# Copying x from the attention tile into the gated layer's ring instead of reading it back from DRAM

## The chip, the cores and the metric

One core of one Trainium2 chip runs the whole kernel. The metric is the device time of one execution in microseconds. TensorE (PE) multiplies matrices, VectorE (DVE), ScalarE (ACT) and GpSimd (POOL) work element by element, SyncE (SP) issues nearly all DMAs. A profile of one execution goes with the times; its line numbers (L508) are those of the kernel file.

## What is computed

```python
# q, k, v: 4 batches x 8 heads x 576 x 64, f: 4 x 8 x 576
cum = np.cumsum(np.log(np.clip(f, 1e-4, 1.0)), axis=-1)
scores = q @ k.T / 8 + cum[:, None] - cum[None, :]       # per head, causal mask
attn = softmax(scores) @ v
x = attn.transpose(0, 2, 1, 3).reshape(2304, 512)
h = (sigmoid(x @ w_gate) * (x @ w_val)) @ w_out           # 512 -> 1536 -> 512
h2 = h @ w_in2                                            # 512 -> 2048
out = (h2 * clip(h2 + 3, 0, 6) / 6) @ w_out2              # 2048 -> 512
```

## The kernel before

**Attention** goes over 16 pairs of heads: 4 batches of 4 pairs. A pair has four units (blocks of query rows), run in the order 1 to 4 in the first seven pairs and 4 to 1 in the later ones. For each unit the main loop issues `scores` (TensorE, L371 and L385), `expo` (VectorE and ScalarE, L392 and L400), one step later `norm` (GpSimd, L437), two steps later `flip` (transposes on TensorE, copies to `etA`, `etB` on ScalarE, L474) and three steps later `values` (TensorE, L494). `values` leaves the pair's x, transposed, 128 rows (two heads) by 576 tokens of one batch, in two SBUF tiles: `x0` the rounded high part (ScalarE, L498), `x1` the low part (VectorE, L499). Each of the two tags has two buffers. `store` then writes both to the DRAM tensors `x_d` (L503).

**The gated layer** works on chunks of 512 tokens (the last has 256). It takes x as four blocks of 128 rows, `xk[kc]` with `kc` 0 to 3. A block is just the x of one pair of heads: pair `hp` of a batch is block `kc = hp`. Every product is made of three matmuls, high x high (L508), high weight x low x (L509), low weight x high x (L510). `load_x` (L206) brings one block of one chunk, high and low part, from `x_d` into the next of six slots of `xr`, a ring in the tile `big`.

While attention runs, `Filler` interleaves part of the gated layer for chunks 0, 1 and 2 (`NCA = 3`): two of the six groups of 256 features (`NGA = 2`). Chunk c lies in batches c-1 and c: its tokens 512c to 512c + 512 begin 64c tokens before batch c does. The main loop calls `fill.load(p.b, p.hp + 1)` two steps after the pair's store, and `Filler.run` starts a chunk when its batch is done:

```python
        if t >= 5:
            p, s = units[t - 5]
            if s == p.order[-1] and t < len(units) + 3:
                fill.load(p.b, p.hp + 1)
```

`Filler.load` holds blocks back where an earlier chunk still needs the ring. After attention the other feature groups follow for all chunks (the second pass, which loads chunks 0 to 2 again from `x_d`), and then the last layer.

**Order.** The loops write the program; the tile framework finds the dependences between accesses of tiles and DRAM tensors, and chooses at build time the order on each engine and queue from a planned timeline (`schedule_with_timeline_sim=True`). On the chip each engine and SP take their instructions in that fixed order. SP issues loads of q, k, v (L264, L268), of the decay (L302), of raw weights (L101), the x stores (L503), the x loads (L206) and the partial sums' stores (L594), and stands still where one has to wait.

Of the kernel before, what the change touches and what calls it, by code (L numbers as in the profile page):

```python
# [7 lines left out]
F32 = mybir.dt.float32  # L8
# [12 lines left out]
def attn_moe_kernel(  # L21
# [13 lines left out]
    nc = tc.nc  # L35
    B, H, S, D = q.shape
# [3 lines left out]
    P = 128  # L40
# [157 lines left out]
    xr = [big[:, 2 * T1 * i : 2 * T1 * i + 2 * T1].rearrange("p (a b) -> p a b", a=2) for i in range(6)]  # L198
    ring = {"x": 0, "g": 0, "s": 0}

    def load_x(src, c, kc):
        t0, T = chunks[c]
        x = xr[ring["x"] % len(xr)][:, :, :T]
        ring["x"] += 1
        for a in range(2):
            nc.sync.dma_start(x[:, a].bitcast(F32), src[a][kc * P : (kc + 1) * P, t0 : t0 + T])  # L206
        return x


# [26 lines left out]
    def row(mm, first):  # L236

        if not first:
            tc.keep_in_program_order(mm)
# [34 lines left out]
    class Pair:  # L274
# [202 lines left out]
        def values(self, part):  # L477


            if self.x is None:  # L480
                self.x = [ax.tile([P, S], F32R, tag=f"x{a}", name="x") for a in range(2)]
            c0, n, nk = (0, 256, 2) if part == 0 else (256, 320, NKT)
            pool, tag = (psF, "F") if FV(self) else (psB, "B")
            o = pool.tile([P, 512], F32, tag=tag, name="pv")[:, :n]
            for kt in range(nk):
                q0 = max(0, kt * P - c0)
                for j in range(2):
                    if part == 0:
                        e = self.etA[:, j, kt * 256 : 256 + kt * P]
                    elif kt < NQ:  # L490
                        e = self.etB[:, j, kt, q0:]
                    else:
                        e = self.etB[:, j, NQ - 1, 0:TAIL]
                    row(nc.tensor.matmul(  # L494
                        o[64 * j : 64 * j + 64, q0:], self.vn[:, kt, j], e, start=(kt == 0), stop=(kt == nk - 1)
                    ), kt == 0 and j == 0)
            xh, xl = (x[:, c0 : c0 + n] for x in self.x)
            nc.scalar.copy(xh, o)  # L498
            nc.vector.tensor_tensor(xl, o, xh.bitcast(F32), ALU.subtract)  # L499

        def store(self):
            for t, d in zip(self.x, x_d):
                nc.sync.dma_start(  # L503
                    d[self.hp * P : (self.hp + 1) * P, self.b * S : (self.b + 1) * S], t.bitcast(F32)
                )
# [38 lines left out]
    class Gated:  # L544
# [6 lines left out]
        def load(self, n):  # L551

            while len(self.xk) < n:
                self.xk.append(load_x(x_d, self.c, len(self.xk)))
# [94 lines left out]
    def layer(src, order, feats, ups, downs, finish, rate, first, more=None):  # L649
# [3 lines left out]
        def load(c, n):  # L653
            while len(loaded[c]) < n:
                loaded[c].append(load_x(src, c, len(loaded[c])))
# [383 lines left out]
    NGA, NCA, GA = 2, 3, 1  # L1039
# [27 lines left out]
    for t in range(len(units) + 3):  # L1067
        if 2 <= t < len(units) + 2:
            p, s = units[t - 2]
            p.flip(s)  # L1070
        if t < len(units):
            p, s = units[t]
            i = p.order.index(s)
            nxt = pairs[p.i + 1] if p.i + 1 < len(pairs) else None
            if i == 0 and nxt:
                nxt.load()
                nxt.load_decay()
                nxt.load_v()
            p.scores(s)
            p.expo(s)  # L1080
            if s > 1:
                p.hide(s - 1)
            if s == 2:
                p.hide(0)
            if nxt and i == (len(p.order) - 1 if p.up else 2):
                nxt.tail_decay()
        if 1 <= t <= len(units):
            p, s = units[t - 1]
            p.norm(s)
        if t < len(units) + 2:  # L1090

            fill.step(16 * (done + 1) + 3 - t + (TL if done == NCA else 0))
        if t >= 3:
            p, s = units[t - 3]
            if s in p.parts:
                p.values(p.parts[s])
            if s == p.order[-1]:
                p.store()
                if p.hp == NP - 1 and p.b < NCA:
                    done = p.b + 1  # L1100
# [5 lines that stand above are left out]
        if t < len(units):  # L1106
            p, s = units[t]
            if p.order.index(s) == max(0, len(p.order) - 3):
                if nxt:
                    nxt.prep()  # L1110
        if t >= C0:
            conv.run(CS if len(conv.jobs) <= 2 * NSA - 6 * NGA else CE if t < 16 else CA, EA)
        fill.n = done
    att.close()
    pace["dve"] = None
    psU = fu.enter_context(tc.tile_pool(name="psU", bufs=4, space=PSUM, reuse_waits="tile"))
# [60 lines left out]
```

## Time and profile before

| | us |
|---|---|
| median of 3 runs | 1041.06 (1040.39 to 1042.2) |
| profiled execution | 1043.08 |
| its span | 1041.0 |
| TensorE busy in it | 1021.1 |
| DVE, ACT, POOL busy | 571.4, 457.0, 307.6 |

The span is the profiled stretch from the first to the last instruction; the time of the execution holds some 2 us around it. Attention takes the first 314 us of it. Busy time of TensorE counts a matmul from its start to its modelled end, and neighbours overlap. A row "A <- B" in a list of waits says that A stood still until B was done.

### The profile page before, as it was taken

What the parts mean: (1) busy time and instruction counts of PE and PEld (TensorE: products, weight loads), DVE (VectorE), ACT (ScalarE), POOL (GpSimd) and SP (SyncE); (2) the same over time, 40 slices, a digit from 0 to 9 for tenths busy, and PEclk for the clock granted to TensorE, in tenths of its full rate; (3) what the DMA queues carried; (4) which work ended last, traced back from release to release, by engine and by line L of the source; (5) the groups of instructions that cost most, each with busy time, mean ns of one, the idle gap of its engine ahead of it and who ended that gap; (6) DMA issues with size and microseconds to landing.
All of it is one profiled execution on the core that took longest, in us unless ns stands there. A gap on an engine that the chain in (4) does not pass through costs nothing.

```text
span 1041.0 us, 15648 instructions
## 1 busy us (share of the span) xinstructions
PE 1021.1 (98%) x5410; PEld 837.0 (80%) x5410; DVE 571.4 (55%) x1282; ACT 457.0 (44%) x1004; POOL 307.6 (30%) x385
## 2 busy tenths in 40 slices
PE   7999999998999999999999999999999999999998
PEld 4656766765768888998888888888998998999997
DVE  5686655445434654456667267665655644443442
ACT  5786466456453443223334134353444432342333
POOL 4577555445432322030234123231111111111110
PEclk9999999999999999999999999999999999999999
DMA  7986666364334435184697458955589632952311
GB/s 184 269 246 196 178 182 180 108 173 116 100 121 139 128 123 158 57 276 176 260 344 244 150 183 293 353 196 211 224 311 338 255 146 79 341 206 81 142 71 61
DMA packets 118319, 197.79 MB, mean 190 GB/s; under 512 B 63648, under 2 KB 68256, under 8 KB 114144
## 3 DMA queue, kind: packets, MB, share of 16 engines
q1 hardware_dynamic: 118144, 196.64, 56.5%
q8 instruction: 43, 0.70, 0.3%
q14 instruction: 36, 0.29, 0.1%
q10 hardware_dynamic: 96, 0.15, 0.0%
HBM read 143.47 MB, written 53.29 MB: 189 GB/s over the span
## 4 chain that ended last, share of the span: by engine, by line
PE 90%; DMA 5%; DVE 2%; issue 1%; POOL 1%; ACT 1%; SPq 0%; POOLq 0%; DVEq 0%; ACTq 0%
PE po L510 11%; PE po L509 11%; PE po L508 11%; PE u L508 5%; PE u L509 5%; PE u L510 5%; PE pg L508 5%; PE pg L509 5%; PE pg L510 5%; PE pv L508 5%; PE pv L509 5%; PE pv L510 5%; PE pv L494 4%; PE st L371 3%; PE tt L461 2%; PE st L385 1%
## 5 line engine op out<-in xcount | busy, mean ns | idle before, releaser
L65 POOL TENSOR_TENSOR big<-tail,big 128x384 fp32r<-128x384 f32 x48 | 49.9, 1039 | 312.8 <-ACT big L62 299.4
L940 ACT ACTIVATE tail<-h,three 128x384 f32<-128x384 f32 x96 | 59.2, 616 | 157.9 <-DVE h L1000 157.0
L510 PE MATMUL po<-w,big 128*128 128x512 f32 x288 | 113.8, 395 | 0.0
L509 PE MATMUL po<-w,big 128*128 128x512 f32 x288 | 113.5, 394 | 0.0
L508 PE MATMUL po<-w,big 128*128 128x512 f32 x288 | 112.0, 389 | 0.0
L1000 DVE TENSOR_TENSOR h<-h,u 128x384 f32<-128x384 f32 x96 | 53.1, 553 | 105.6 <-PE u L510 103.2
L437 POOL TENSOR_SCALAR e<-e,m 128x256 f32<-128x256 f32 (+4 forms) x144 | 87.9, 624 | 62.1 <-DVE m L435 30.3
L400 ACT ACTIVATE e<-e,m 128x256 f32<-128x256 f32 (+4 forms) x144 | 83.7, 583 | 40.8 <-DVE m L392 35.7
L508 PE MATMUL pg<-big,wg 128*128 128x512 f32 (+1 forms) x240 | 89.0, 374 | 4.1 <-DMA big<-x_d 4.1
L509 PE MATMUL pg<-big,wg 128*128 128x512 f32 (+1 forms) x240 | 89.7, 375 | 0.1
L508 PE MATMUL pv<-big,wv 128*128 128x512 f32 (+1 forms) x240 | 89.4, 372 | 0.0
L510 PE MATMUL po<-big,wo 128*128 128x512 f32 (+1 forms) x240 | 88.9, 372 | 0.0
L510 PE MATMUL pv<-big,wv 128*128 128x512 f32 (+1 forms) x240 | 88.9, 370 | 0.0
L509 PE MATMUL pv<-big,wv 128*128 128x512 f32 (+1 forms) x240 | 88.9, 370 | 0.0
L510 PE MATMUL pg<-big,wg 128*128 128x512 f32 (+1 forms) x240 | 88.9, 370 | 0.0
L509 PE MATMUL po<-big,wo 128*128 128x512 f32 (+1 forms) x240 | 88.7, 370 | 0.0
L508 PE MATMUL po<-big,wo 128*128 128x512 f32 (+1 forms) x240 | 88.5, 374 | 0.0
L721 DVE SCALAR_TENSOR_TENSOR sg<-sg,pv 128x512 f32<-128x512 f32 (+1 forms) x48 | 29.6, 618 | 94.6 <-PE pv L510 78.9
L111 ACT ACTIVATE raw<-raw 128x512 f32<-128x512 f32 x68 | 45.6, 682 | 59.6 <-DVE raw L108 58.2
L392 DVE CUSTOM_DVE_ANT_0 e<-st,dc 128x384 f32<-128x384 f32 (+3 forms) x110 | 53.7, 519 | 30.8 <-PE st L371 19.0
L941 DVE SCALAR_TENSOR_TENSOR tail<-tail,h 128x384 f32<-128x384 f32 x96 | 54.6, 569 | 23.6 <-ACT tail L940 23.5
L62 ACT CAST big<-tail 128x384 fp32r<-128x384 f32 x96 | 48.9, 510 | 34.4 <-DVE tail L941 34.2
(147 smaller groups left out, 2326.5 us busy)
## 6 DMA issues: line engine op xcount, KB each, us to landing
h<-xc_d SPq DMA_DIRECT2D x21, 768.0 KB, 6.4
big<-x_d SPq DMA_DIRECT2D x56, 256.0 KB, 3.9
raw<-in_moe_w_out_dram SPq DMA_DIRECT2D x28, 512.0 KB, 4.4
h<-wt_d SPq DMA_DIRECT2D x12, 1024.0 KB, 4.9
big<-wt_d SPq DMA_DIRECT2D x12, 1024.0 KB, 5.4
dc<-cum_d SPq DMA_DIRECT2D x16, 576.0 KB, 5.0
x_d<-x SPq DMA_DIRECT2D x32, 288.0 KB, 3.5
h<-wb_d SPq DMA_DIRECT2D x12, 768.0 KB, 4.8
```

Of the source, the lines that this page charges most:

```text
L62: nc.scalar.copy(hi, src)
L65: eng_lo.tensor_tensor(lo, src, hi.bitcast(F32), ALU.subtract)
L111: nc.scalar.activation(e, e, AF.Copy, scale=2.0**-112)
L392: i = nc.vector.tensor_tensor_reduce(out=e, in0=st, in1=d, op0=ALU.add, op1=ALU.min, scale=1.0, scalar=init, accum_out=m[:, a : a + 1],)
L400: nc.scalar.activation(e, e, AF.Exp, bias=m[:, a : a + 1], scale=-1.0, accum_out=m[:, 4 + b : 5 + b])
L437: nc.gpsimd.tensor_scalar(e, e, m[:, 12 + j : 13 + j], 1.0, ALU.mult, ALU.mult)
L508: nc.tensor.matmul(o, wh, xh, start=first, stop=False)
L509: nc.tensor.matmul(o, wh, xl, start=False, stop=False)
L510: nc.tensor.matmul(o, wl, xh, start=False, stop=last)
L940: nc.scalar.activation(sg, h, AF.Relu, bias=three, scale=1.0)
L941: nc.vector.scalar_tensor_tensor(sg, sg, 6.0, h, ALU.min, ALU.mult)
L1000: pace["dve"] = tt(c, a, o, ALU.add)
```

## The change

`store` notes the pair's two tiles in a dictionary `fresh` under (batch, pair), for batches 0 to 2. `load_x` looks there for (chunk, block). If it finds the tiles, the columns of the chunk that lie in batch c are copied by DMA out of the tiles, SBUF to SBUF, and only the 64c columns of the batch before are loaded from `x_d`; for chunk 0 there are none. Without an entry it loads as before. When a pair takes new x tiles, all entries but the last are dropped; after attention the dictionary is cleared. The stores to `x_d` stay.

```diff
+    fresh = {}
+
     def load_x(src, c, kc):
         t0, T = chunks[c]
         x = xr[ring["x"] % len(xr)][:, :, :T]
         ring["x"] += 1
-        for a in range(2):
-            nc.sync.dma_start(x[:, a].bitcast(F32), src[a][kc * P : (kc + 1) * P, t0 : t0 + T])
+        here = fresh.get((c, kc))
+        n = T if here is None else c * S - t0
+        if n:
+            for a in range(2):
+                nc.sync.dma_start(x[:, a, :n].bitcast(F32), src[a][kc * P : (kc + 1) * P, t0 : t0 + n])
+        if here is not None:
+            for a in range(2):
+                nc.sync.dma_start(x[:, a, n:].bitcast(F32), here[a][:, : T - n].bitcast(F32))
         return x
...
             if self.x is None:
+                for key in list(fresh)[:-1]:
+                    del fresh[key]
                 self.x = [ax.tile([P, S], F32R, tag=f"x{a}", name="x") for a in range(2)]
...
         def store(self):
+            if self.b < NCA:
+                fresh[self.b, self.hp] = self.x
             for t, d in zip(self.x, x_d):
...
+    fresh.clear()
     att.close()
```

## Rows read from the trace of the kernel before

**Rows 1.** The page, first part: busy time of each engine, share of the span.

```profile
PE 1021.1 (98%) x5410; PEld 837.0 (80%) x5410; DVE 571.4 (55%) x1282; ACT 457.0 (44%) x1004; POOL 307.6 (30%) x385
```

**Rows 2.** Waits of TensorE: us in total, times, longest.

```profile
PE pg L508 <- DMA big<-x_d: 4.1, 3, 2.7
```

**Rows 3.** Windows of 20 us: length, busy time by engine, clock, DMA share, GB/s.

```profile
220.00:240.00 20.00, 17.25 (x108) 12.05 (x109) 7.35 (x34) 11.13 (x32) 9.49 (x17) 1.00 0.64 183
240.00:260.00 20.00, 17.90 (x117) 12.26 (x116) 12.47 (x50) 14.38 (x43) 11.05 (x18) 1.00 0.46 123
...
320.00:340.00 20.00, 20.00 (x90) 16.54 (x89) 12.35 (x20) 8.98 (x16) 6.60 (x4) 1.00 0.27 89
```

**Rows 4.** The chain that ended last, in order: start us, us, what.

```profile
162.11 2.73 DMA x_d<-x
164.90 2.75 DMA big<-x_d
...
228.73 4.88 DMA x_d<-x
233.67 2.68 DMA big<-x_d
...
246.12 3.35 DMA x_d<-x
249.49 4.79 DMA big<-x_d
```

**Rows 5.** TensorE's timeline at the three places; in brackets, idle before.

```profile
166.14 0.92 PE L371 MATMUL st<-kp,qp 64*128 64x384 f32 x4
167.69 0.73 PE L508 MATMUL pg<-big,wg 128*128 128x512 f32 x2 [0.63 <-DMA big<-x_d]
...
232.74 0.92 PE L371 MATMUL st<-kp,qp 64*128 64x384 f32 x4
236.40 0.73 PE L508 MATMUL pg<-big,wg 128*128 128x512 f32 x2 [2.75 <-DMA big<-x_d]
...
249.60 0.92 PE L371 MATMUL st<-kp,qp 64*128 64x384 f32 x4
251.29 0.73 PE L508 MATMUL pg<-big,wg 128*128 128x512 f32 x2 [0.77 <-DMA big<-x_d]
```

**Rows 6.** SP at L206: its waits, and its issues (ns min/median/max).

```profile
SPq L206 <- DMA x_d<-x: 26.8, 25, 3.4
...
L206 SPq DMA_DIRECT2D big<-x_d x64: 319/372/2463, 39.7 to 585.4; - x64
```

**Rows 7.** SP's timeline: start us, us, what was issued.

```profile
163.13 0.41 SPq L264 DMA_DIRECT2D vn<-in_v_dram  x1
...
228.73 0.93 SPq L503 DMA_DIRECT2D x_d<-x  x2
229.75 0.45 SPq L264 DMA_DIRECT2D vn<-in_v_dram  x1
...
239.38 0.61 SPq L268 DMA_DIRECT2D vn<-in_v_dram  x1
```

**Rows 8.** DMA issues: KB each, median us from issue to landing.

```profile
big<-x_d SPq DMA_DIRECT2D x56, 256.0 KB, 3.9
...
x_d<-x SPq DMA_DIRECT2D x32, 288.0 KB, 3.5
...
kn<-in_k_dram SPq DMA_DIRECT2D x16, 32.0 KB, 2.7
```

**Rows 9.** Landing times: stores L503 at 228.7, loads L206 at 78.5 us.

```profile
DMA to landing us min/median/max: 4.9/4.9/4.9
...
DMA to landing us min/median/max: 5.8/5.9/5.9
```

**Rows 10.** Windows at 229 us, TensorE alone; last columns DMA share, GB/s.

```profile
229.00:231.00 2.00, 2.00 (x15) 1.00 1.16 356
231.00:233.66 2.66, 2.65 (x17) 1.00 0.60 190
```

## The prediction

> **What bounds the kernel now.** I read the page's first part first: TensorE is busy 98% of the span [rows 1], so nothing shortens this kernel but fewer or shorter waits of TensorE, and all of them together are 1041.0 - 1021.1 = 19.9 us. The list of TensorE's waits came next. The largest entry is this change's own subject: the first gate product L508 waits 4.1 us, in 3 places, for `big`, loaded from `x_d` [rows 2]. The windows of 20 us show that TensorE is full once attention has ended (20.00 of 20.00 in the last row) and leaves 2.75 and 2.10 us open in the two stretches from 220 to 260 us, where the last two pairs of batch 2 finish [rows 3]. So time given back there goes through to the end: the work behind it is TensorE's own.
>
> The chain that ended last says how the waits come about [rows 4]. Three times it runs store, then load, then gate product: at 162 us (I call it place A, chunk 1, last pair of heads), at 228 us (B, chunk 2, third pair) and at 246 us (C, chunk 2, last pair). The load is issued when the store has landed. TensorE's timeline shows the price: its last score product ends at 166.14 + 0.92 = 167.06, and L508 starts at 167.69, so A costs 0.63; B costs 2.75 (free at 233.66, start 236.40), C 0.77 (free at 250.52, start 251.29) [rows 5]. The sum is 4.15, the 4.1 of the list.
>
> **The change, part by part.** *Removed:* for the 12 pairs of batches 0 to 2, the load's wait for the landing of the store. The loads are L206; on SP they sat 26.8 us, 25 times, behind stores [rows 6]. The store itself stays, since the second pass and chunk 3 read `x_d`. A full-width load of each pair becomes a copy out of the tile; that 24 loads less of DRAM are read I cost at nothing, since no TensorE wait but those three names the x tensor.
>
> *Added:* chunk 1 takes 64 columns, chunk 2 takes 128, of the batch before from DRAM. That makes 8 pairs x 2 = 16 more DMAs of 32 and 64 KB. SP's price for one lies between 0.32 us, the shortest issue of L206 [rows 6], and 0.61 us, the issue of a 32 KB load of v [rows 7]; two cost 0.64 to 1.22. The code writes them ahead of the copies. They need only old DRAM data and a free ring slot, so they may go ahead of the stores and then cost nothing; behind the stores they delay the copies by all of that. What SP issues next are loads for later pairs and raw weights, and TensorE waits for none of them in these places.
>
> *Moved:* when the copy can go. It needs the x tile complete, as the stores do, and it comes after them on SP: two stores take 0.93, the load of v that stood between 0.41 to 0.45 [rows 7]. No transfer from SBUF to SBUF is in the trace, so I bound its landing by the loads and stores of about its size: medians 3.9 and 3.5 us, a 32 KB load 2.7 [rows 8]. The end for an idle queue is 2.7 (places A and B, load: the chain's second row of each [rows 4]); the end for a loaded one is 4.9, what both stores at B took [rows 9]. I lean to the first at A and C and near the second at B.
>
> At A the stores are issued until 162.11 + 0.93 = 163.04 and v until about 163.54. The copy goes out between 163.0 and 164.8 (with pieces), lands 2.7 later at 165.7 to 167.5, and TensorE is free at 167.06: 0 to 0.4 of the wait stays. I take a gain of 0.5 of 0.63.
>
> At B v ends at 229.75 + 0.45 = 230.2, the pieces end by 231.4. The queue was over-full until 231 and 60% busy after it [rows 10]; the copy is behind stores that landed at 233.6 and 234.15. 256 KB at the 356 GB/s of the full stretch take 0.74 us, so I put the first copy at 234.15 + 0.74 = 234.9. The ends are 230.2 + 2.7 = 232.9 (no wait left) and 231.4 + 4.9 = 236.3 (0.1 gained). With 234.9 the wait is 1.2 and the gain 1.5.
>
> At C the second store is issued at 246.12 and, by half of the 0.93, until some 246.6. The copy goes out between 246.6 and 248.2 (v and two pieces later) and lands 2.7 to 3.35 later (the short end, and this store's own [rows 4]), at 249.3 to 251.6 against 250.52: a gain of 0 to 0.77, I take 0.5.
>
> Sum: 0.5 + 1.5 + 0.5 = 2.5 us, with ends 0.3 and 4.15.
>
> The Trainium skill (DMA: Bandwidth & Descriptors, "Rules for kernel authors") speaks against the split: it says that transfers under 64 KB pay mostly overhead and should be joined into one. The row of the 32 KB load agrees, 2.7 us for an eighth of the bytes that take 3.9. With the page's fixed cost of about 2.0 us in series before each copy the sum would, as an estimate, fall to about 0.3 us.
>
> The copy's source tile is held longer. The stores at A and B are three pairs apart, 66.6 us [rows 4], so a pair takes 22 us; the tile is written again by the next pair but one, more than one pair later. A copy that lands within 6 us delays nothing.
>
> **What the order may do.** The order on each engine is planned at build time from assumed readiness. The planner has to be rerun on other dependences, so L508 may go further forward on TensorE, in front of score products that now stand ahead of it. The waits of A, B and C are by how much the chip was later than the plan. If the plan moves L508 by the whole time saved, each wait is back and the gain is 0. If the freed matmuls fill the holes that remain, the other waits in the two open stretches (2.75 + 2.10 - 2.75 - 0.77 = 1.3 us [rows 3, 5]) go too and the gain is up to 4.15 + 1.3 = 5.5. I keep 2.5, between these ends.
>
> **Rivals.** (1) *The queue eats the gain.* The pieces are issued behind the stores and the copies queue behind both, or the plan moves L508 forward and only the later place of the wait changes. For it: B's stores needed 4.9 us and the DMA queue was full. Against it: at A the load landed in 2.75 us, and 0.6 to 0.8 us are enough at A and C. Gain 0.3 by the lower ends: 1040.8 us. The skill's rule on small transfers, above, would give the same.
>
> (2) *Slower: gate products ahead of the scores.* There are four places where the last tile of a chunk is awaited soon: A, B, C and chunk 0's end at 78.5 us, where the load needed 5.8 to 5.9 us [rows 9] and TensorE did not wait. If the plan now counts on one short transfer and puts L508 before the score products of the next pair, TensorE, which takes its instructions in order, stands still with attention behind it. With B's 2.75 us at all four, 11.0 in place of 4.15, the time is 1041.06 + 6.85 = 1047.9 us. It decides against the change from a mean wait of 4.15 / 4 = 1.04 us per place. For it: the waits before show the plan too early three times out of four. Against it: with one transfer in place of two, less can be late.
>
> (3) *The copy is not used*, because the tile has left `fresh` before the load is written out: same time, 1041.06. Against it: load follows store within 5 us at all three places [rows 4], far less than a pair's 22 us, so I give it little.
>
> **Numbers.** The profiled execution took 1043.08 us with a span of 1041.0, 2.0 above the median of 1041.06; the gain is a difference of waits inside the span and is taken off the median: 1041.06 - 2.5 = 1038.6 us. A measurement of this kernel can tell about 0.2%, 2.1 us, from no change. The forecast (gain 1.0 to 5.5, mostly over 2.1) has a chance of 0.50 to be faster by more than that; the low part of it, rival 1 and rival 3 (0.02) make 0.31 for the same; rival 2 and smaller losses by a new order 0.19. The likeliest case alone spans 1035.6 to 1040.1. The range goes from 1035.4 (all waits gone and the holes filled) up to 1043.1 (0.2% above the median), which leaves out some 0.04 below and most of rival 2's 0.19 except its smallest losses.
>
> **What would show it.** In the trace after, the L206 copies start within 2 us of their pair's stores in all 12 pairs, and there are 16 more L206 issues. The list of TensorE's waits has `big` at 1.0 to 2.2 us in place of 4.1, the chain no longer has a store followed by a load in batches 1 and 2, and the stretch after attention starts about 2.5 us sooner. It is wrong if L508's waits are at or above 4.1 (rival 2, or 1 if they only moved), if the copies take 5 us or more at A or C, or if TensorE's other waits in 0 to 320 us grow by more than the three shrink.

## The result and the profile after

| | before | after |
|---|---|---|
| median of 6 runs each, us | 1042.45 (1040.39 to 1045.05) | 1049.42 (1047.28 to 1051.28) |
| profiled execution, its span | 1043.08, 1041.0 | 1048.5, 1046.7 |
| mean granted clock of TensorE | 1.0 | 0.997 |

The kernel became slower by about 7.0 us, a ratio of 1.0067 (95% interval 1.0051 to 1.0084). The forecast of 1038.6 and its range up to 1043.1 were wrong.

Start where the prediction looked: TensorE's waits in the profile after (us in total, times, longest us), against [rows 2].

```profile
PE tt L460 <- POOL e L445: 2.4, 1, 2.4
PE pg L520 <- DMA big<-x: 2.2, 2, 1.1
...
PE tt L463 <- POOL e L445: 0.5, 1, 0.5
...
PE tt L469 <- POOL e L445: 0.4, 1, 0.4
```

The first gate product, now L520, waits 2.2 us in two places where it waited 4.1 in three, the upper end of the forecast (1.0 to 2.2). New are the other three lines, 3.3 us: transposes (`flip`) that wait for GpSimd's normalization (`norm`, L445). In sum, however, TensorE stands still no longer than before: 1046.7 - 1027.1 = 19.6 us of the span, against 19.9. What grew is its busy time, from 1021.1 us [rows 1] to 1027.1 for the same 5410 matmuls:

```profile
PE 1027.1 (98%) x5410; PEld 838.9 (80%) x5410; DVE 575.8 (55%) x1282; ACT 456.8 (44%) x1004; POOL 306.7 (29%) x385
```

So part of the same work took longer. The windows of the profile after say where (length, busy time of PE, PEld, DVE, ACT, POOL, granted clock, DMA share, GB/s; 1.00 is 2.4 GHz, 0.50 is 1.2 GHz). The first line is the end of attention before, the others are after:

```profile
300.00:320.00 20.00, 20.00 (x132) 14.36 (x131) 5.82 (x21) 9.72 (x27) 5.65 (x9) 1.00 0.45 155
...
220.00:240.00 20.00, 18.92 (x117) 13.06 (x114) 8.82 (x41) 11.77 (x36) 9.06 (x16) 1.00 0.65 186
240.00:260.00 20.00, 18.76 (x118) 13.37 (x117) 11.73 (x44) 13.59 (x43) 11.66 (x19) 1.00 0.47 138
300.00:320.00 20.00, 16.71 (x100) 9.59 (x101) 6.32 (x23) 9.28 (x27) 6.48 (x11) 0.83 0.31 100
320.00:340.00 20.00, 20.00 (x90) 16.55 (x89) 9.51 (x15) 7.04 (x12) 6.14 (x3) 1.00 0.25 78
...
308.00:310.00 2.00, 0.15 (x2) 0.00 (x0) 1.04 (x3) 2.00 (x8) 0.00 (x0) 0.98 0.59 175
310.00:312.00 2.00, 0.94 (x3) 0.59 (x4) 0.72 (x1) 0.46 (x1) 1.85 (x4) 0.50 0.50 171
312.00:314.00 2.00, 2.00 (x9) 0.83 (x9) 0.00 (x0) 0.48 (x1) 1.92 (x3) 0.50 0.00 0
314.00:316.00 2.00, 2.00 (x12) 1.01 (x10) 0.00 (x0) 0.00 (x0) 0.27 (x1) 0.50 0.34 26
316.00:318.00 2.00, 2.00 (x16) 1.11 (x13) 0.49 (x1) 0.88 (x2) 0.00 (x0) 0.81 0.64 237
```

The two stretches around B and C are fuller than in [rows 3] (18.92 and 18.76 against 17.25 and 17.90). The stretch in which attention ends, which was full before, has a hole, and after it TensorE runs at half clock until some 316.7. A window that reads "2.00 busy" at clock 0.50 does about half the work that it seems to do: the 20 value matmuls in the next fence take 4.32 us there, and 2.28 before.

TensorE's timeline shows what stands there. After:

```profile
299.23 0.40 PE L522 MATMUL po<-big,wo 128*128 128x512 f32 x1
...
305.17 0.93 PE L379 MATMUL st<-kp,qp 64*128 64x128 f32 x8
306.02 0.66 PE L469 MATMUL tt<-ident,e 128*128 128x128 f32 x4
307.04 1.11 PE L469 MATMUL tt<-ident,e 128*128 128x128 f32 x6 [0.36 <-POOL e L445]
310.57 0.47 PE L460 MATMUL tt<-ident,e 128*128 128x128 f32 x1 [2.43 <-POOL e L445]
311.53 0.69 PE L463 MATMUL tt<-ident,e 128*128 128x128 f32 x2 [0.48 <-POOL e L445]
312.01 0.42 PE L460 MATMUL tt<-ident,e 128*128 128x128 f32 x1
312.37 4.32 PE L504 MATMUL pv<-etB,vn 128*64 128x320 f32 x20
...
317.03 1.50 PE L504 MATMUL pv<-etA,vn 128*64 128x256 f32 x8
318.46 0.50 PE L520 MATMUL pg<-big,wg 128*128 128x512 f32 x1
```

The same stretch before (no row of the prediction comes from it):

```profile
303.36 0.93 PE L371 MATMUL st<-kp,qp 64*128 64x128 f32 x8
304.22 0.50 PE L510 MATMUL po<-big,wo 128*128 128x512 f32 x1
...
307.08 0.39 PE L510 MATMUL po<-big,wo 128*128 128x512 f32 x1
307.39 0.87 PE L494 MATMUL pv<-etA,vn 128*64 128x256 f32 x8
308.20 1.94 PE L461 MATMUL tt<-ident,e 128*128 128x128 f32 x14
...
310.94 2.28 PE L494 MATMUL pv<-etB,vn 128*64 128x320 f32 x20
313.04 0.82 PE L494 MATMUL pv<-etA,vn 128*64 128x256 f32 x8
313.80 0.50 PE L508 MATMUL pg<-big,wg 128*128 128x512 f32 x1
```

Before, 13 output matmuls of chunk 2 (`po`, 304.22 to 307.39, 3.17 us) stand behind attention's last scores. While TensorE does them, VectorE, ScalarE and GpSimd bring the last softmax to the transposes. After, the last `po` is at 299.23: all of chunk 2's output was done before the last scores, and nothing is left to do beside the softmax.

The sum: from the end of the last scores to the second pass it takes 318.46 - 306.10 = 12.36 us after and 313.80 - 304.29 = 9.51 before. Three things that stood behind the last scores before stand ahead of them after: the 13 `po` (3.17 us), 8 value matmuls (307.39 to 308.20, 0.81) and 4 of the 14 transposes behind those (some 0.55), 4.53 in all. The remaining work took 4.98 before, so 12.36 - 4.98 = 7.4 us are lost. Of these, 0.36 + 2.43 + 0.48 = 3.27 are standing still, and 4.1 are slower work: 2.04 for the 20 value matmuls at half clock (4.32 in place of 2.28), 0.68 for the last 8 (1.50 for 0.82), the rest mostly for the transposes, some of which ran at half clock. The last 8 are not the clock's: it was back at 316.7, and in a run below they take 1.50 us at clock 1.00 as well. Why they are slower was not found out.

The last scores themselves end 1.81 us later with 4.53 us more work ahead of them, so the part up to there had become 2.7 us shorter; against a second profile of the kernel before (below, where the last scores end at 302.30) it is 0.7. The second pass starts 4.66 us later. The spans differ by 5.7; the last 1.1 come in small steps at 533 us (0.5) and at 687 to 692 us (0.6), far from attention.

Where did the `po` go? At C the order changed. The timeline after:

```profile
248.32 0.73 PE L520 MATMUL pg<-big,wg 128*128 128x512 f32 x2
248.89 0.39 PE L521 MATMUL pg<-big,wg 128*128 128x512 f32 x1
...
252.97 0.47 PE L520 MATMUL pv<-big,wv 128*128 128x512 f32 x1
...
255.91 0.93 PE L379 MATMUL st<-kp,qp 64*128 64x128 f32 x8
```

L520 starts right behind the scores, with no wait. In the plan made anew the other gate products (248.89 to 249.9) stand ahead of attention's values, and 12 gate-value matmuls (the gated layer's value products, from 252.97) ahead of the next scores. Before, the low part of x landed at 254.28 (the last of [rows 4]), and the other gate products and the gate-value matmuls came later:

```profile
254.32 0.50 PE L509 MATMUL pg<-big,wg 128*128 128x512 f32 x1
...
256.32 0.93 PE L371 MATMUL st<-kp,qp 64*128 64x128 f32 x8
...
257.26 0.48 PE L508 MATMUL pv<-big,wv 128*128 128x512 f32 x1
```

Chunk 2's filler runs early from there on and is used up 50 us later. At A and B the order is as before; the waits there are 1.10 and 1.08 us. In chunk 0's products, from 84 to 135 us, the order changed as well; the first experiment shows what that is worth.

### The profile page after: what moved, and what is told of

Read it like the earlier page. It is cut to its first block, busy times and chain, and to the rows that moved or that the text cites. A ratio compares the mean times of both kernels' runs of the same rounds, so it can differ in the third digit from the quotient of the medians.

```text
span 1046.7 us, 15664 instructions
## 1 busy us (share of the span) xinstructions
PE 1027.1 (98%) x5410; PEld 838.9 (80%) x5410; DVE 575.8 (55%) x1282; ACT 456.8 (44%) x1004; POOL 306.7 (29%) x385
## 4 chain that ended last, share of the span: by engine, by line
PE 89%; DMA 6%; DVE 3%; ACT 1%; issue 0%; SPq 0%; POOL 0%; DVEq 0%; ACTq 0%
PE po L522 11%; PE po L521 11%; PE po L520 10%; PE u L520 5%; PE u L521 5%; PE u L522 5%; PE pg L520 5%; PE pv L520 5%; PE pv L521 5%; PE pg L521 5%; PE pv L522 5%; PE pg L522 5%; PE pv L504 4%; PE st L379 3%; PE tt L469 2%; PE st L393 2%
## 5 line engine op out<-in xcount | busy, mean ns | idle before, releaser
L520 PE MATMUL po<-w,big 128*128 128x512 f32 x288 | 112.0, 389 | 0.0
L445 POOL TENSOR_SCALAR e<-e,m 128x256 f32<-128x256 f32 (+4 forms) x144 | 86.9, 618 | 58.4 <-DVE m L443 30.2
L520 PE MATMUL pg<-big,wg 128*128 128x512 f32 (+1 forms) x240 | 89.4, 375 | 2.3 <-DMA big<-x 2.2
L520 PE MATMUL pv<-big,wv 128*128 128x512 f32 (+1 forms) x240 | 89.5, 373 | 0.0
L520 PE MATMUL po<-big,wo 128*128 128x512 f32 (+1 forms) x240 | 88.6, 374 | 0.0
```

Source lines behind the costliest of these rows:

```text
L445: nc.gpsimd.tensor_scalar(e, e, m[:, 12 + j : 13 + j], 1.0, ALU.mult, ALU.mult)
L520: nc.tensor.matmul(o, wh, xh, start=first, stop=False)
```

## The experiments

"C" is the copy of the last pair of batch 2 into chunk 2. Each group of experiments was timed beside the kernel before, whose medians were 1042.28 to 1043.22 us; every ratio is against that of its own group.

**Which copy does it?** Two kernels split the change: all copies but C's, and C's alone.

```diff
-            if self.b < NCA:
+            if self.b < NCA and (self.b, self.hp) != (NCA - 1, NP - 1):
                 fresh[self.b, self.hp] = self.x
...
-            if self.b < NCA:
+            if (self.b, self.hp) == (NCA - 1, NP - 1):
                 fresh[self.b, self.hp] = self.x
```

> All copies stay but those of the last pair of batch 2 (place C), which loads from x_d as before. Hole theory (the loss lies at the end of attention, where chunk 2's products are used up before the last softmax and the clock falls; the copy at C is what moved them forward): no hole, granted clock 1.00 in the window from 300 to 320 us, A and B as in the changed kernel (waits 1.1 + 1.1 in place of 0.63 + 2.75), so about 1042.4 - 1.2 = 1041.2 us. Transfer theory (copies and extra pieces cost by themselves, on SP or in the DMA queue): 22 of 24 copies and 14 of 16 pieces are still there, so 0.9 of the loss of 7.0 us: 1048.7 us.

> Only the last pair of batch 2 (place C) is copied, all others load from x_d: two copies and two pieces in all. Hole theory: the hole at the end of attention is there with clock 0.5 for some 6 us, and the gains at A and B are not: 1049.4 + 1.2 = 1050.6 us. Transfer theory: 1/12 of 7.0 us: 1043.0 us.

All but C: 1043.56 us, 1.0009 (0.9996 to 1.0023), no hole. C alone: 1050.45 us, 1.0073 (1.0052 to 1.0093), with the hole (the mean clock of 0.91 makes some 3.5 us at 0.50, by estimate, where some 6 were expected). Their windows, all but C first, then C alone:

```profile
300.00:320.00 20.00, 20.00 (x128) 15.03 (x125) 5.13 (x17) 8.49 (x23) 5.05 (x8) 1.00 0.48 165
```

```profile
300.00:320.00 20.00, 16.56 (x106) 9.74 (x105) 6.26 (x26) 10.49 (x31) 7.39 (x12) 0.91 0.35 122
```

Two copies and two small loads out of 24 and 16 carry the whole loss. The other 22 copies cost nothing that can be measured, and bring nothing that can be: the 1.2 us that the expectation took off for A and B did not show. TensorE's order fits. With all copies but C's it is that of the kernel before except from 84 to 135 us, so the changed order there is not the loss; with C's alone it is that of the kernel before up to 252 us, and from there on no `po` is left behind the last scores.

**Is it the missing filler?** The whole change, with the last output product of chunk 2 (12 matmuls) kept behind the score products that precede it in the program; `mm` is the score matmul just written:

```diff
+                        pace["pe"] = mm
...
-                down(po, self.wo, self.gs, es)
+                with tc.issue_after(pace["pe"].ins) if self.c == NCA - 1 and e >= KC - 1 else ExitStack():
+                    down(po, self.wo, self.gs, es)
```

> The changed kernel, and the last of chunk 2's four output products (12 matmuls, 2.8 us) may not be issued on TensorE before the last score products of attention. Hole theory: it fills most of the 3.3 us of the hole, the clock stays at 1.00, and the 3.3 + 3.2 us come back: 1049.4 - 6.5 = 1042.9 us or less. Transfer theory: nothing changes, 1049.4 us.

1041.95 us, 0.9993 (0.998 to 1.0006): all of the loss is gone, with the same copies and transfers. The second pass starts at 311.50, and the window is

```profile
300.00:320.00 20.00, 19.56 (x118) 14.33 (x115) 5.90 (x23) 8.49 (x25) 6.50 (x11) 1.00 0.46 152
```

**How much of it is the clock?** 20 matmuls whose result nobody reads, behind the last scores, keep TensorE at work in the hole without doing any of the kernel's work (`pace` is set as in the run above):

```diff
     list(fill.groups)
+    with tc.issue_after(pace["pe"].ins):
+        for _ in range(20):
+            o = psF.tile([P, 512], F32, tag="F", name="o")
+            nc.tensor.matmul(o[:, : 3 * P], identb, masks, start=True, stop=True)
```

> The changed kernel with 20 extra matmuls (bf16, 384 columns, result never read) allowed from the last score products on, so that TensorE has something to do in the hole but no work of the kernel is done sooner. If the clock is half of the loss at the hole, it stays at 1.00 and 3.2 us come back: 1049.4 - 3.2 = 1046.2 us. If the idle time alone is the loss: 1049.4 us. If the transfers are the loss: 1049.4 us, with the clock at 1.00.

1046.54 us, 1.0037 (1.0023 to 1.005), clock 1.0:

```profile
300.00:320.00 20.00, 19.71 (x132) 12.22 (x131) 6.35 (x24) 9.61 (x27) 6.98 (x11) 1.00 0.36 126
```

Useless work makes the kernel 1049.42 - 1046.54 = 2.9 us faster than the change alone, so some 2.9 of the 7.0 us are the clock. In the trace it takes 316.77 - 306.82 = 9.95 us from the last scores to the second pass, 2.4 less than with the change alone. The 20 value matmuls are back at their time of before, and the last 8 are not:

```profile
312.49 2.27 PE L505 MATMUL pv<-etB,vn 128*64 128x320 f32 x20
...
315.34 1.50 PE L505 MATMUL pv<-etA,vn 128*64 128x256 f32 x8
```

The other 4.1 are mostly time without useful work (the 20 matmuls fill some 4 us). Of the 2.7 us between the two profiled executions (1048.5 and 1045.8) 1.7 show at the start of the second pass (316.77 against 318.46; the last scores end 0.7 later in this one) and 1.0 later, in the small steps named above, which are not the clock's.

**Would a later C undo the early order?** Only C's two copies wait until the pair's stores have landed:

```diff
-                nc.sync.dma_start(x[:, a, n:].bitcast(F32), here[a][:, : T - n].bitcast(F32))
+                cp = nc.sync.dma_start(x[:, a, n:].bitcast(F32), here[a][:, : T - n].bitcast(F32))
+                if (c, kc) == (NCA - 1, KC - 1):
+                    tc.add_manual_dep(
+                        cp.ins, stored[c, kc][a].ins.name,
+                        mybir.DependencyInfo(mybir.DependencyClass.Sync, mybir.DependencyReason.DATA), reason="after store",
+                    )
```

> The changed kernel, but the copies of the last pair of batch 2 (place C) may go only when that pair's stores have landed; they still come out of the tile. If the order moved because the x of C counts as ready earlier, the order falls back part of the way (9 of chunk 2's last output matmuls stand behind the first of the last score products instead of none, where the kernel before has 13 behind all of them): the hole is smaller, 1045 us, between 1043 and 1048. If the source in SBUF or the pieces cost by themselves, 1049.4 us as in the changed kernel.

A miss: 1051.88 us, 1.0074 (1.0052 to 1.0096). The waits of its TensorE (its line numbers are 6 higher at L526, 5 at L465 and L450):

```profile
PE tt L465 <- POOL e L450: 3.8, 1, 3.8
PE pg L526 <- DMA big<-x: 3.4, 2, 2.9
```

It has both holes: 2.9 us at C, where the clock falls to 0.50 too, and 3.8 at the end of attention. Nine `po` matmuls were left in its last stretch (306.43 to 308.36), but the plan put them ahead of the last scores (310.06), where they cover nothing of the softmax behind those. Late filler was of no use in itself; it has to stand behind the last scores. The order fell back only part of the way (in the kernel before, 18 `po` stand behind the scores of 298.26, which are the ones before the last). So the copy at C makes the plan change, but that it does so only by making x ready earlier is not shown: with the copy made to wait for the stores, as the load had, the plan was still not the old one.

**Copies ahead of the stores, alone and with filler held.** `store` calls `fill.load` before it issues the stores; then the same with one, and with two, output products held.

```diff
                 fresh[self.b, self.hp] = self.x
+                fill.load(self.b, self.hp + 1)
             for t, d in zip(self.x, x_d):
```

> The changed kernel with the copies written ahead of the pair's stores to x_d, so that they don't queue behind 576 KB of stores on SP and in the DMA queue. If the waits left at A and B (1.1 + 1.1 us) are that queue's, they go to about 0.2 in sum; the hole at the end of attention stays as it is: 1049.4 - 2.0 = 1047.4 us. If the copies' landing has nothing to do with the stores: 1049.4 us.

> Copies ahead of the stores, and the last output product of chunk 2 held behind the last score products, as in the run with the hold alone (1041.95 us). Hole theory: no hole, and the waits of A and B gone: 1041.95 - 1.6 = 1040.3 us, 0.2% faster than the kernel before. If a wait saved at A and B is only waited for elsewhere in attention: 1041.9 us.

> Copies ahead of the stores, and two output products of chunk 2 (24 matmuls, 5.5 us) held behind the last score products instead of one. If one product was not enough for the hole (0.4 us of TensorE's time stayed open from 300 to 320 us), 0.3 us more come back: 1040.2 us. If the second product is missing earlier, before the last scores, it is slower than with one: 1041.5 us.

Copies first: 1047.09 us, 1.0037 (1.0024 to 1.0051). The wait of the first gate product is 0.3 us in total, and the hole at the end is there (16.57 busy in 300 to 320). With one product held: 1040.49, 0.9974 (0.9961 to 0.9987). With two: 1038.88, 0.9958 (0.9933 to 0.9983), the fastest version by its median and 1.3 us faster than expected. No wait for x is left among its TensorE's largest; its second pass starts at 309.83:

```profile
300.00:320.00 20.00, 20.00 (x112) 15.84 (x112) 4.43 (x16) 7.11 (x19) 4.99 (x8) 1.00 0.48 165
```

**How firm is the 4.15 us that the prediction summed?** The kernel before once more.

> The kernel before, for a second profile of it: how much the waits at A, B and C (0.63, 2.75, 0.77 us) vary between executions. If they are the plan's lateness against a loaded DMA queue, their sum is within 1 us of 4.1 and the largest is at B; if they are chance, it is not.

1040.67 us, and TensorE's wait is

```profile
PE pg L508 <- DMA big<-x_d: 2.2, 3, 1.2
```

The expected 4.1 was missed: half of it had been a slow landing in that one execution. B was again the largest, 1.17; the first store there landed 3.4 us after its issue, where it had taken 4.9 [rows 9].

**All of chunk 2's products held** behind the score products ahead of them in the program (gate, value and output, in the manner of the one above).

> The changed kernel, and no product of chunk 2 (gate, value or output) may be issued on TensorE before the score products that stand ahead of it in the program; before it, the planner moved them forward as far as their x allowed. All 48 output matmuls then stand behind the score products of the last unit but one, 45 of them behind the last. Hole theory: there is more than enough work behind the last scores, so no wait for the normalization and clock 1.00 in the window from 300 to 320 us; the products are missing from 250 to 300 us instead, where each unit's softmax may now open small holes: 1041 to 1045 us, 1043. Transfer theory: 1049.4 us.

1039.29 us, 0.9967 (0.9947 to 0.9986), 3.7 us faster than expected. That it ends the hole was forecast (300 to 320 is full, clock 1.00); why it beats the version with one product held was not found out. Its profiled execution, 1042.56, is one of its three slowest; it has a hole of 1.73 us at A and the clock down behind it.

**What makes the fastest version fast?** The two halves of its edit apart: two products held in the kernel before, and two held in the change with its copies behind the stores. The diff is the one above with `e >= KC - 2`.

> The kernel before, without any copy, with the last two output products of chunk 2 (24 matmuls) kept behind the scores that precede them in the program. The kernel before already has 13 output matmuls behind its last scores. Theory A, the gain of the version with copies ahead of the stores and two products held comes from both edits: without the copies this one stays within 1.5 us of the kernel before, ratio 0.9985 to 1.0015. Rival B, holding alone gives the gain: ratio about 0.996, 4 us faster.

> The change with its copies behind the stores, and two output products held in place of one. Theory A: holding one product brought 1041.95; the second adds at most the 0.4 us that the last wait on GpSimd still cost, so about 1041.5, ratio 0.997 to 1.000, because the waits for x at two places (2.2 us after the change) stay. Rival B, the second product is what gives the gain: ratio about 0.996, as with the copies ahead.

The first: 1042.08 us, 0.999 (0.9976 to 1.0003). The second: 1041.76, 0.9989 (0.9974 to 1.0003). Holding alone brings nothing that can be told from no change, and copies first alone lose 0.37%. Of these two edits only both together gain, 0.42%. The ends of the intervals of the second and of the fastest just overlap, so their difference of 2.9 us is likely rather than certain. Nor is copying first the only way: the version with all of chunk 2's products held gains 0.33% with its copies behind the stores, and cannot be told from the fastest. What the two have in common was not found out.

## Why the prediction was wrong

**What bounds the kernel** was right in that TensorE is busy 98% before and after. That "nothing shortens this kernel but fewer or shorter waits of TensorE" leaves out that its busy time can grow: the waits came to 19.9 us before and 19.6 after, and the busy time of the same matmuls rose by 6.0. And the list of waits tells where cover is missing now, not where it is thin. The stretch from 304 to 314 us held no wait before, so no row pointed at it.

**Removed, added and the pieces** were right. There are 16 more x loads and copies on SP (56 and 24 for 64). The pieces went out far ahead, the last of chunk 1's at 122 to 125 us for A at 162, the last of chunk 2's at 199 to 201 us for B at 230 and C at 244, and no wait of TensorE's names them. So what the Trainium skill says of transfers under 64 KB (DMA: Bandwidth & Descriptors, "Rules for kernel authors") did no harm here, though the pieces did land in 2.3 and 3.4 us for 32 and 64 KB, near the 3.2 of a 256 KB copy: issued early, that time is hidden. The estimate of 0.3 us, for pieces in series before each copy, was not put to the test.

**Moved** sized the landings well. The chain of the profile after has the copies where the loads of [rows 4] were:

```profile
162.70 4.42 DMA big<-x
...
230.38 3.85 DMA big<-x
```

At B the copy landed at 234.23, forecast 234.9, and 1.08 of the wait stayed, forecast 1.2. At C nothing stayed, forecast 0.3. At A it landed at 167.12, within the 165.7 to 167.5, but TensorE was free at 166.16, 0.9 earlier, so 1.10 stayed in place of 0.1. One row was misread: at C the load of [rows 4] is the low part of x, landed at 254.28; L508 had waited for the high part, until 251.29. The base was mis-sized, too: 4.15 in the profiled execution, 2.2 in the next one, 3.7 in that of the kernel before with two products held; and the median taken off, 1041.06 of 3 runs, became 1042.45 with 6. Without the hole the change is worth 0.4 us (1041.95 against 1042.38), which can't be told from no change; a gain of 2.5 lies outside that version's interval.

**"What the order may do" is the step that failed.** It let the plan move L508 forward and gave that a gain between 0 and 5.5, "the waits of A, B and C" and "the holes that remain". It looked for the effect only where the moved products go to, and put the place that they leave at nothing. What counts is where they are taken from: 3.17 us of filler left the one stretch where nothing else covers the softmax, and 7.4 us were lost there. The split by pair, the held product and the useless matmuls show this one by one: C's copy alone makes the loss, one product held ends it, and keeping TensorE busy gives back the part of the clock. Why the planner orders chunk 2 anew as it does stays open.

**Rival 2** had the right sign, products ahead of scores as the right cause and, at 1047.9, nearly the size. The size was luck, since its mechanism did not happen: it had TensorE waiting for a late x at four places, and x was on time at C, the place where the order changed. Rival 1 (a gain of 0.3) comes near what is left without the hole (0.4), and not the time. Rival 3 was excluded by the trace, which has 24 copies. Of the prediction's signs of being right, the stretch after attention did not start 2.5 us sooner but 4.66 later; of its signs of being wrong, none came up. The nearest was that TensorE's other waits in 0 to 320 us grow by more than the three shrink. The three shrank by 4.15 - 2.2 = 1.95; the others grew by 3.27 at the end of attention, but by only some 1.2 in all, since waits earlier in attention had become shorter. The loss was in slower work, which no sign asked for.

## What to carry to other kernels

A changed dependence makes a build-time plan place its filler anew, and can pull it forward. Filler has a second job: it covers the last latency of the stage it fills. Before forecasting such a change, look at the last link of the latency-bound stage (here scores, softmax, transposes), count the matmuls that stand behind it, and ask whether they will still be there; if in doubt, pin a few of them. Read the granted clock by window along with the busy time, compare the busy time of the same work and not the waits alone, and take the size of a DMA wait from more than one execution.

## What the runs showed of the hardware

- A hole can cost about twice its length: 3.27 us of standing still at the end of attention, and 2.4 (by the trace) to 2.9 us (by the medians) more that useless matmuls in its place gave back. The granted clock was 0.50 from 310 to some 316.7 us, though TensorE was busy from 312. The Trainium skill (TensorE: Matmul & The Clock Gate, "What's actually happening") has the same two levels, full and half.
- The length of a hole alone does not decide it. At B in the kernel before TensorE stood still for 2.75 us and the clock stayed at 1.00; at A in the version with all products held it fell to 0.50 (170 to 172 us) behind 1.73 us. The two windows of 2 us behind the start of each hole, before and then that version:

```profile
234.00:236.00 2.00, 0.00 (x0) 0.00 (x0) 1.07 (x6) 2.00 (x7) 0.50 (x2) 1.00 0.56 182
236.00:238.00 2.00, 1.60 (x10) 0.86 (x12) 0.41 (x2) 0.33 (x2) 2.00 (x4) 1.00 0.21 82
```

```profile
168.00:170.00 2.00, 1.75 (x8) 0.98 (x10) 1.69 (x7) 1.72 (x6) 1.62 (x3) 0.79 0.00 2
170.00:172.00 2.00, 2.00 (x10) 0.84 (x9) 1.02 (x1) 0.16 (x1) 2.00 (x4) 0.50 0.00 0
```

- What decides between the two was not found out. The mean clock goes with part of the spread: the runs of the version with all products held whose mean clock was 0.999 or 1.0 took 1038.06 to 1039.8 us, the three at 0.997 or 0.998 took 1041.43 to 1044.17.
- A copy from SBUF to SBUF landed in about the time of a load or store of its size. By size, the copies (L214) landed in medians of 3.2 us (256 KB), 3.9 (224 KB) and 3.6 (192 KB), where loads of 256 KB before took 3.9 and stores of 288 KB 3.5 [rows 8]. One issue took 0.61 us in the median on SP, against 0.38 for a load of x in the same execution.
